# A seven-product first matmul for the third row group of a convolution and MLP kernel

## The chip, the cores and the metric

The kernel runs on one core of one Trainium2 chip. The metric is the device time of one execution in microseconds (us), as the median of the runs. In the profile the engines are called PE (TensorE, matmul), PEld (TensorE's weight load), DVE (VectorE), ACT (ScalarE), POOL or Pool (GpSimd) and SP (SyncE).

## The reference

The input x has shape (8, 4224, 192) in float32. First, a causal convolution with 7 taps runs along the sequence; the taps are a softmax over the kernel axis, one set for each of 8 heads of 24 channels. Its output is then normalised and sent through a two-layer MLP with a residual:

```python
w = exp(weight - max(weight)); w = w / (sum(w) + 1e-9)        # (8 heads, 7 taps)
y[b, s, h, :] = sum over k of w[h, k] * x_pad[b, s + k, h, :]  # 6 zero rows ahead of the sequence
xn  = (y - mean(y)) / sqrt(var(y) + 1e-6) * g_ln               # over the 192 channels
out = y + max(xn @ w_ch1, 0) @ w_ch2                           # 192 -> 768 -> 192
```

## The kernel before

**Rows and groups.** A partition holds 32 consecutive rows of a sequence (the rows that are left over, 8 on every partition, form one group over all sequences). The work goes through groups of up to 16 rows a partition. Group 0 has 6 rows, group 1 the 8 left-over rows, group 2 (the third group) 10 rows, and each later group 16. All pools that matter here have one or two buffers, so groups overlap only where the order of instructions lets them. The order is written by hand: each engine executes its instructions in the order of the source (`tc.manual_schedule()`), and semaphores keep the data dependencies.

**The convolution.** `load_x(g)` fetches a group with six rows of lead. `first_tap` multiplies by tap 0 on ACT into `y`, `second_tap` multiplies by tap 1 on ACT into `tb`, and `add_second_tap` adds `tb` onto `y` with accumulating DMAs issued by Pool. `conv` does the remaining taps on DVE (L417), one instruction for each tap and head: a multiply-add of 24 channels by the rows of the group, 384 elements a partition for 16 rows. `transpose` (L428) turns `y` in blocks of 32 into `yt`, `moments` (L448) takes the statistics on DVE, and `root` computes the inverse deviations on Pool with 22 small operations. The deviation is applied after the second matmul, since it commutes with the ReLU; the mean is taken out of `w1` beforehand.

**Two matmuls in float32.** "Up" multiplies by `w1` (192 x 768) and "down" by `w2` (768 x 192). Up contracts over 32 channels a row group of PE, four row groups side by side, each with a PSUM bank of its own (`rows_of_tiles`, L533). PSUM has 8 banks; `take_set` hands out banks 0-3 or 4-7 in turn and `take_bank` single ones, both from one counter.

Groups 0 and 1 do both matmuls plainly (`up`, and `down` with L772 and the evictions L783/L786). Groups 3 and later use Winograd's form of Strassen's scheme in both: the operands are cut into quarters, sums of quarters are formed, and seven products replace eight. `up_mixed` does this for up: `sums_of_y` forms the sums of quarters of `yt` (s1, s2 on DVE, s3 and s4 on Pool, where s4 overwrites the quarter a21), `w1sums` holds the sums of quarters of `w1`, and the parts c11, c12, c21, c22 of the hidden layer are evicted from PSUM by ACT (L642) and completed by accumulating DMAs (`add_by_dma`, L609), by a DVE addition that reads PSUM (L648) and by ReLUs on ACT (L655). `down_fast` does it for down (L835): the half sums on DVE (L802), evictions on ACT (L841), and a list `work` of ACT instructions that are put behind the matmul chunks; `behind` says how many go behind each chunk of each product. `finish_fast` adds and transposes the result back (L897, L899).

Group 2 before the change does up plainly, in six chunks of 128 hidden units with an eviction each (L523), and down with `down_fast`. Around it, before the change, the source orders (stage g is the turn of the main loop):

- Stage 0, behind the statistics: Pool forms `w1sums[1]` and `w1sums[0]` (L582).
- Stage 1: `conv(2, 2)` on DVE, the transposition of group 2, `first_tap(3)`, the DMAs of group 3's second taps (6 heads), the four `w2sums` on Pool, `load_x(4)` and `store_y(2)` by Pool, then `down(1)`; then the statistics of group 2, its `root` on Pool, and `conv(3)` for heads 6 and 7.
- Stage 2: `up(2)`, with the scaling of group 0's outputs, the accumulating output DMAs of groups 0 and 1 (`add_to_out`) and the first taps of group 4 put between its chunks (`between`); then `conv(3)` for heads 0 to 5, `lower_sum(2)` between two parts of it, `w1sums[2]` on Pool, and `down_fast(2)`. In there DVE transposes group 3 and subtracts two quarters of `w1` in place (L870).

`let_in` writes one element of a tile on DVE; whatever writes that tile next on Pool waits for it, so Pool starts there no earlier than DVE has come to that place.

`room` is one large tile that holds the hidden layer (`ht`) of all groups in turn, and at its end the second taps of group 3 (`tb[3]`).

Of the kernel before, what the change touches and what calls it, by code (L numbers as in the profile page):

```python
# [16 lines left out]
def kernel(  # L17
# [69 lines left out]
    FC = NF // 2  # L87

# [295 lines left out]
    def second_tap(g, heads=(0, H)):  # L384
# [7 lines left out]
        elif g == 3:  # L392
            tb[g] = room[:, (NF * NQ * C - D) * J :].rearrange("p (j d) -> p j d", d=D)
        else:
            tb[g] = bpool.tile([P, J, D], F32, tag="tb", name=f"tb{g}")
# [97 lines left out]
    def hidden_tile(g):  # L493
        n = groups[g][2]

        if fast[g]:
            ht[g] = room.rearrange(
# [41 lines left out]
    def between(g, f):  # L539

        if g == 1 and f > 2:
            second_tap(3, heads=[(0, 2), (2, 5), (5, 6)][f - 3])
        elif g == 2:
            if f == 0:
                scale(0, 0, groups[0][2])
                add_to_out(0, 0, groups[0][2])
                nc.gpsimd.memset(xg[4][0:1, 0:PAD, :], 0.0)
            elif f == 2:
                add_to_out(1, 0, groups[1][2])
            elif f > 2:  # L550
                first_tap(4, heads=[(0, 3), (3, 6), (6, 7)][f - 3])
# [34 lines left out]
    def quarters_of_y(g):  # L586
        if width(g) == C:
            cuts = [(slice(HJ * h, HJ * h + HJ), slice(0, C)) for h in range(2)]
# [4 lines left out]
    def sums_of_y(g, engine):  # L593

        room = upool.tile([P, 3 * HJ * CH * C], F32, tag="ys", name=f"ysums{g}")
        room = room.rearrange("p (v j c t) -> p v j c t", v=3, c=CH, t=width(g))
# [11 lines left out]
    def add_by_dma(dst, src):  # L608
        nc.gpsimd.dma_start(out=dst, in_=src, accum_op=ALU.add)  # L609

# [195 lines left out]
    def lower_sum(g, fs=range(FC)):  # L806

        a = of_products(g)
        if g in MIXED:
# [8 lines left out]
    def down_fast(g, work):  # L818
# [9 lines left out]
        banks = [take_bank() for c in range(CH) for i in range(2)]  # L828
# [22 lines left out]
        if g == 2:  # L851
            work += [lambda h=h: first_tap(4, heads=(h, h + 1)) for h in range(7, H)]
# [6 lines left out]
        behind = (1, 1, 1, 1) if g == 2 else (3, 2, 2, 3)  # L859
# [6 lines left out]
        if g + 1 < NG:  # L866
            transpose(g + 1)
            if g == 2:
                b11, b12 = quarters_of_w1()[0:2]
                nc.vector.tensor_tensor(b12, b12, b11, op=ALU.subtract)  # L870
# [3 lines left out]
        for c in range(CH):  # L874
# [3 lines left out]
            )  # L878
        product(0, a[:, 1, 1], w2sums[:, 1], parts[0], False, 2)
# [111 lines left out]
    for g in range(NG):  # L991
# [3 lines left out]
        if mixed:  # L995
            work = up_mixed(g, ahead(g), pending)
            pending = iter(())
        else:
            up(g)
            work = []  # L1000
        if g == 0:
# [17 lines left out]
            sums_of_quarters(w1sums[:, 0], w11, w1sums[:, 1])  # L1019
            next(root(0, True))  # L1020
        elif g == 1:
            conv(2, 2)
            transpose(2)
            first_tap(3)
            add_second_tap(3, 6)
# [65 lines left out]
```

## Time and profile before

| what | value |
|---|---|
| median of 3 runs | 958.18 us (957.67 to 958.47) |
| the profiled execution's own time | 959.62 us |
| its span in the profile | 957.5 us |
| PE busy | 950.6 us (99%) |
| DVE busy | 890.7 us (93%) |
| ACT busy | 696.6 us (73%) |
| Pool busy | 338.4 us (35%) |
| granted PE clock | 1.0 throughout |
| first matmul of group 2 | 81.64 to 101.23 us |
| second matmul of group 2 | 101.23 to 118.67 us |

The profiled execution took 959.62 us, of which the profile's span covers 957.5; the other 2.1 lie around it. All positions in the span are in us from its start. A row of the timeline gives start, duration, engine, source line, operation, output and inputs, shape and how often; what stands in brackets is how long the engine was idle before it and who ended that. The duration of a group runs from the first start to the last end, and neighbouring instructions overlap a little, so a step's price is taken from start to start. A float32 matmul appears as two records, so a round of four row groups is 8 records.

### The profile page before, as it was taken

To read this page: it belongs to the slowest core of one execution; us is meant where nothing else is said; L and a number is where in the kernel's file an instruction comes from. 1 tells how busy PE (TensorE), PEld (TensorE's weight loads), DVE (VectorE), ACT (ScalarE), POOL (GpSimd) and SP (SyncE) were. 2 spreads that over 40 slices of the span, in tenths; PEclk is the share of its full clock that TensorE was granted. 3 is DMA by queue.
4 is the path that set the end of the run, shared out by engine and by line. 5 is a ranking of instruction groups with operands and counts; after the bars stand their busy time and mean duration, and the time that the engine had idled before them with its cause. 6 is when DMAs were issued, how large, how long until landed. Compare 5 with 4: busy or idle time off the path is not lost.

```text
span 957.5 us, 37878 instructions
## 1 busy us (share of the span) xinstructions
PE 950.6 (99%) x16858; PEld 743.1 (78%) x16858; DVE 890.7 (93%) x1489; ACT 696.6 (73%) x1165; POOL 338.4 (35%) x472
## 2 busy tenths in 40 slices
PE   9999999999999999999999999999999999999998
PEld 8998896876869697787968778695867769586787
DVE  7999999999999998999999999999999999999757
ACT  6853678596877959687795968779695877967462
POOL 1058422623145141533227141452316232261310
PEclk9999999999999999999999999999999999999999
DMA  8359589689697988979697896969889696778251
GB/s 204 101 160 212 98 230 280 121 187 229 135 263 138 249 156 181 224 132 277 127 249 151 196 220 127 278 131 252 155 197 205 124 276 132 175 136 138 42 96 68
DMA packets 39544, 168.82 MB, mean 176 GB/s; under 512 B 4437, under 2 KB 8150, under 8 KB 33367
## 3 DMA queue, kind: packets, MB, share of 16 engines
q0 software_dynamic: 32576, 106.25, 59.8%
q1 hardware_dynamic: 6800, 60.16, 17.3%
q8 instruction: 132, 2.16, 0.9%
q14 instruction: 30, 0.25, 0.1%
q10 hardware_dynamic: 6, 0.00, 0.0%
HBM read 38.93 MB, written 50.33 MB: 93 GB/s over the span
## 4 chain that ended last, share of the span: by engine, by line
PE 97%; POOL 1%; DMA 1%; ACT 0%; issue 0%; DVE 0%; ACTq 0%; POOLq 0%
PE ps L533 47%; PE ps L835 44%; PE ps L772 4%; PE ps L367 1%; DMA room<-room 1%; PE ps L326 1%; ACT room L642 0%; POOL room L609 0%; POOL d L460 0%; PE ps L354 0%; POOL r L483 0%; POOL d L479 0%; DVE yt L428 0%; POOL d L478 0%; PE ps L335 0%
## 5 line engine op out<-in xcount | busy, mean ns | idle before, releaser
L417 DVE SCALAR_TENSOR_TENSOR y<-xg,taps,y 128x384 f32<-128x384 f32 (+3 forms) x720 | 364.8, 583 | 1.9 <-DMA y<-room 1.3
L835 PE MATMUL ps<-room,w2sums 128*32 128x256 f32 (+2 forms) x4608 | 247.4, 371 | 0.0
L533 PE MATMUL ps<-yt,w 32*128 32x256 f32 (+2 forms) x4104 | 234.8, 378 | 0.3 <-DVE yt L428 0.3
L642 ACT COPY room<-ps 128x1024 f32<-128x1024 f32 (+1 forms) x135 | 175.0, 1296 | 78.6 <-PE ps L533 77.8
L533 PEld LDWEIGHTS ps<-yt,w 32*128 32x128 f32 x4104 | 204.1, 185 | 25.8 <-issue 8.7
L835 PEld LDWEIGHTS ps<-room,w2sums 128*32 128x32 f32 x4608 | 153.5, 110 | 87.8 <-ACT room L655 5.3
L835 PE MATMUL ps<-room,w 128*32 128x256 f32 (+2 forms) x3456 | 189.8, 371 | 0.1
L802 DVE TENSOR_TENSOR room<-room 128x1024 f32<-128x1024 f32 (+2 forms) x147 | 161.2, 1172 | 22.7 <-PE ps L835 16.1
L835 PEld LDWEIGHTS ps<-room,w 128*32 128x32 f32 x3456 | 113.9, 110 | 67.9 <-DVE room L648 5.0
L533 PE MATMUL ps<-ysums,w1sums 32*128 32x256 f32 x2160 | 125.3, 379 | 0.2 <-issue 0.2
L533 PEld LDWEIGHTS ps<-ysums,w1sums 32*128 32x128 f32 x2160 | 109.1, 185 | 11.2 <-ACT room L642 3.6
L925 POOL DMA_DIRECT2D out_dram<-ot x69 | 58.9, 940 | 159.3 <-ACT ot L914 102.6
L409 POOL DMA_DIRECT2D y<-tb x59 | 52.4, 1384 | 155.0 <-ACT room L841 110.2
L841 ACT COPY cs<-ps 128x256 f32<-128x256 f32 (+2 forms) x192 | 70.2, 367 | 45.6 <-PE ps L835 45.5
L655 ACT ACTIVATE room<-room 128x1024 f32<-128x1024 f32 (+1 forms) x89 | 92.5, 1072 | 0.8 <-DMA room<-parts_cs 0.8
L914 ACT ACTIVATE ot<-ot,r 128x192 f32<-128x192 f32 x224 | 90.9, 464 | 0.0
L380 ACT ACTIVATE y<-xg,taps 128x384 f32<-128x384 f32 (+3 forms) x141 | 73.1, 608 | 0.2 <-DMA xg<-in_x_dram 0.2
L448 DVE BATCH_NORM_STATS2 st<-y 128x6 f32<-128x192 f32 x264 | 70.1, 344 | 0.0
L841 ACT COPY room<-ps 128x256 f32<-128x256 f32 (+2 forms) x96 | 35.5, 369 | 46.5 <-PE ps L835 43.8
L398 ACT ACTIVATE tb<-xg,taps 128x384 f32<-128x384 f32 (+1 forms) x120 | 66.0, 627 | 0.0
L533 PE MATMUL ps<-yt,w1sums 32*128 32x256 f32 x1080 | 65.3, 380 | 0.4 <-ACT room L642 0.4
L533 PE MATMUL ps<-ysums,w 32*128 32x256 f32 x1080 | 64.6, 376 | 0.0
(113 smaller groups left out, 918.0 us busy)
## 6 DMA issues: line engine op xcount, KB each, us to landing
xg<-in_x_dram SPq DMA_DIRECT2D x14, 2112.0 KB, 16.6
room<-room POOLq DMA_DIRECT2D x45, 512.0 KB, 5.1
out_dram<-ot POOLq DMA_DIRECT2D x59, 384.0 KB, 9.6
y<-tb POOLq DMA_DIRECT2D x58, 384.0 KB, 8.5
out_dram<-y SPq DMA_DIRECT2D x13, 1536.0 KB, 9.5
room<-parts_cs POOLq DMA_DIRECT2D x28, 512.0 KB, 6.8
room<-parts_tb POOLq DMA_DIRECT2D x14, 1024.0 KB, 7.6
xg<-in_x_dram POOLq DMA_DIRECT2D x1, 2112.0 KB, 13.6
```

The source lines that it names most:

```text
L380: nc.scalar.mul(y[g][:, 0:n, cs], xg[g][:, 0:n, cs], taps[:, h, 0:1])
L398: nc.scalar.mul(tb[g][:, 0:n, cs], xg[g][:, 1 : 1 + n, cs], taps[:, h, 1:2])
L417: nc.vector.scalar_tensor_tensor(out=y[g][:, 0:n, cs], in0=t[:, k : k + n, cs], scalar=taps[:, h, k : k + 1], in1=y[g][:, 0:n, cs], op0=AL ...
L448: nc.vector.bn_stats(out=sums[g][:, j, :], in_=y[g][:, j, :])
L533: nc.tensor.matmul(banks[:, q, i * w : i * w + w], right[rows, c, P * i : P * i + P], left[rows, :, c, :], start=(first and c == 0 and i = ...
L642: nc.scalar.activation(dst, src, AF.Relu) if relu else nc.scalar.copy(dst, src)
L655: nc.scalar.activation(c, c, AF.Relu)
L802: nc.vector.tensor_tensor(a[:, *dst, f], a[:, *left, f], a[:, *right, f], op=op)
L835: nc.tensor.matmul(dst[C * q : C * q + C, 0:w], right[:, f, C * c : C * c + C], left[:, f, q], start=(first and f == PAIR), stop=(f == PAI ...
L841: nc.scalar.copy(to[:, c], dst[:, 0:w].rearrange("p (j t) -> p j t", t=t))
L914: nc.scalar.mul(ots[g][:, j, :], ots[g][:, j, :], rstd[g][:, j : j + 1])
L925: nc.gpsimd.dma_start(out=rows[:, d0:d1], in_=src[:, d0:d1], accum_op=ALU.add)
```

## The change

The change gives group 2 a first matmul of seven products (`up_whole`) and orders the work around it anew:

- `up_whole(2)` replaces `up(2)`. Each half of the rows has 5 rows, so a product is 160 columns wide. Its parts are evicted by ACT; c11 and c22 are completed by one accumulating DMA each, c21 by an addition on DVE that reads PSUM. Group 4's memset, `root(2)`, the output DMAs of groups 0 and 1, the first taps of group 4 and parts of `conv(3)` stand between the products.
- The sums of quarters it needs: `w1sums[2]` is formed on DVE in stage 0 instead of on Pool in stage 2; the in-place subtraction of `w1` quarters goes from DVE in `down_fast(2)` to Pool in stage 1; `sums_of_y(2)` is new in stage 1.
- In stage 1, Pool's first three `w2sums` are let in at the transposition, ahead of the second taps' DMAs, and the fourth goes to the end; the DMAs carry 5 heads instead of 6, and the scaling of group 0's outputs comes ahead of `down(1)`.
- Group 3's transposition in `down_fast(2)` is done in two parts, the second behind the half sums; the banks of `down_fast` are assigned in another order; `behind` is (1, 1, 2, 2) for group 2.
- The hidden layer of group 2 lies at another place of `room` (FROM_2), and `tb[3]` is smaller.

```diff
+    FROM_2 = 2 * FC * NQ * J * T - FC * NQ * (J - 6) * C
...
         elif g == 3:
-            tb[g] = room[:, (NF * NQ * C - D) * J :].rearrange("p (j d) -> p j d", d=D)
+            tb[g] = room[:, NF * J * P - n * 5 * GRP :].rearrange("p (j d) -> p j d", d=5 * GRP)
...
         if g == 1 and f > 2:
-            second_tap(3, heads=[(0, 2), (2, 5), (5, 6)][f - 3])
-        elif g == 2:
-            if f == 0:
-                scale(0, 0, groups[0][2])
-                add_to_out(0, 0, groups[0][2])
-                nc.gpsimd.memset(xg[4][0:1, 0:PAD, :], 0.0)
-            elif f == 2:
-                add_to_out(1, 0, groups[1][2])
-            elif f > 2:
-                first_tap(4, heads=[(0, 3), (3, 6), (6, 7)][f - 3])
+            second_tap(3, heads=[(0, 2), (2, 4), (4, 5)][f - 3])
...
+    def up_whole(g):
+        n = groups[g][2] // 2
+        w = n * C
...
+        Y, X = take_set(), take_set()
...
+        def close(c, banks, pool, tag):
+            part = pool.tile([P, J * D], F32, tag=tag, name=f"parts_{tag}{g}")
+            part = part[:, 0 : FC * NQ * w]
+            nc.scalar.copy(part.rearrange("p (f q w) -> p f q w", f=FC, q=NQ), seen(banks))
+            add_by_dma(c.rearrange("p f q w -> p (f q w)"), part)
+
+        def relu(c, f):
+            nc.scalar.activation(c[:, f], c[:, f], AF.Relu)
+
+        rows_of_tiles(X, a11, b11, True, False, True)
+        nc.scalar.copy(c11, seen(X))
+        rows_of_tiles(Y, a12, b21, True, True, True)
+        close(c11, Y, cpool, "cs")
+        nc.gpsimd.memset(xg[4][0:1, 0:PAD, :], 0.0)
+        rows_of_tiles(X, s2, t[0], False, False, True)
+        nc.scalar.copy(c21, seen(X))
+        rows_of_tiles(Y, s3, t[1], True, False, True)
+        nc.scalar.copy(c22, seen(Y))
+        first_tap(4, heads=(0, 1))
+        rows_of_tiles(X, s1, b12, False, False, True)
+        close(c22, X, bpool, "tb")
+        next(root(2, True))
+        for k in range(2):
+            add_to_out(k, 0, groups[k][2])
+        first_tap(4, heads=(1, 2))
+        rows_of_tiles(Y, a22, t[2], False, True, True)
+        conv(3, 2, 5, heads=(0, 5))
+        conv(3, 5, 6, heads=(0, 3))
+        nc.vector.tensor_tensor(c21, c21, seen(Y), op=ALU.add)
+        rows_of_tiles(X, s4, b22, False, True, True)
+        for f in (PAIR, *range(PAIR)):
+            relu(c11, f)
+        nc.scalar.activation(c12, seen(X), AF.Relu)
+        lower_sum(g, (PAIR, *range(PAIR)))
+        conv(3, 5, 6, heads=(3, 5))
+        conv(3, 6, K, heads=(0, 5))
+        work = [lambda h=h: first_tap(4, heads=(h, h + 1)) for h in range(2, 5)]
+        work += [lambda f=f: relu(c22, f) for f in (PAIR, *range(PAIR))]
+        return work + [lambda h=h: first_tap(4, heads=(h, h + 1)) for h in range(5, H)]
...
-        banks = [take_bank() for c in range(CH) for i in range(2)]
+        banks = [take_bank() for i in range(2 * CH)]
+        banks = [banks[c + CH * i] for c in range(CH) for i in range(2)]
...
-        behind = (1, 1, 1, 1) if g == 2 else (3, 2, 2, 3)
+        behind = (1, 1, 2, 2) if g == 2 else (3, 2, 2, 3)
...
-        if g + 1 < NG:
+        if g == 2:
+            transpose(g + 1, 0, CH)
+        elif g + 1 < NG:
             transpose(g + 1)
-            if g == 2:
-                b11, b12 = quarters_of_w1()[0:2]
-                nc.vector.tensor_tensor(b12, b12, b11, op=ALU.subtract)
...
+        if g == 2:
+            transpose(g + 1, CH, NC)
         product(0, a[:, 1, 1], w2sums[:, 1], parts[0], False, 2)
...
             sums_of_quarters(w1sums[:, 0], w11, w1sums[:, 1])
+            nc.vector.tensor_tensor(w1sums[:, 2], w21, w1sums[:, 0], op=ALU.subtract)
             next(root(0, True))
         elif g == 1:
             conv(2, 2)
+            let_in(w2sums[:, 2])
             transpose(2)
             first_tap(3)
-            add_second_tap(3, 6)
+            scale(0, 0, groups[0][2])
             sums_of_quarters(w2sums[:, 2], b12, b22)
             sums_of_quarters(w2sums[:, 0], b12, b11)
             sums_of_quarters(w2sums[:, 1], b22, w2sums[:, 0])
-            sums_of_quarters(w2sums[:, 3], b21, w2sums[:, 1])
+            add_second_tap(3, 5)
             load_x(4, nc.gpsimd, pad=False)
             store_y(2, nc.gpsimd)
-        elif g == 2:
-            conv(3, 2, 5, heads=(0, 6))
-            lower_sum(2)
-            conv(3, 5, K, heads=(0, 6))
-            let_in(w1sums[:, 2])
-            sums_of_quarters(w1sums[:, 2], w21, w1sums[:, 0])
+            sums_of_y(2, nc.gpsimd)
+            moments(2)
+            sums_of_quarters(w12, w12, w11)
+            sums_of_quarters(w2sums[:, 3], b21, w2sums[:, 1])
         if g < 2:
             down(g)
             if g == 1:
-                moments(2)
-                next(root(2, True))
-                conv(3, heads=(6, H))
+                conv(3, heads=(5, H))
             continue
```

More of the change, by code (lines that the diff above doesn't have):

```diff
@@ L496, in hidden_tile @@
         if fast[g]:
-            ht[g] = room.rearrange(
+            start = 0 if g in MIXED else FROM_2
+            ht[g] = room[:, start : start + NF * NQ * n * C].rearrange(
                 "p (h e f q j t) -> p h e f q j t", h=2, e=2, f=FC, q=NQ, t=width(g)
@@ L587, in quarters_of_y @@
         if width(g) == C:
-            cuts = [(slice(HJ * h, HJ * h + HJ), slice(0, C)) for h in range(2)]
+            n = groups[g][2] // 2
+            cuts = [(slice(n * h, n * h + n), slice(0, C)) for h in range(2)]
         else:
@@ L595, in sums_of_y @@
         room = upool.tile([P, 3 * HJ * CH * C], F32, tag="ys", name=f"ysums{g}")
+        room = room[:, 0 : 3 * groups[g][2] // 2 * CH * C]
         room = room.rearrange("p (v j c t) -> p v j c t", v=3, c=CH, t=width(g))
@@ L609, in add_by_dma, with seen @@
         nc.gpsimd.dma_start(out=dst, in_=src, accum_op=ALU.add)
+    def up_whole(g):
+        n = groups[g][2] // 2
+        w = n * C
+        assert FC * w <= 512
+        hidden_tile(g)
+        a = of_products(g)
+        (c11, c12), (c21, c22) = [
+            [a[:, h, e].rearrange("p f q j t -> p f q (j t)") for e in range(2)] for h in range(2)
+        ]
+        a11, a12, a21, a22 = quarters_of_y(g)
+        s1, s2, s3, s4 = ysums[g]
+        b11, b12, b21, b22 = quarters_of_w1()
+        t = [w1sums[:, k] for k in range(3)]
+        Y, X = take_set(), take_set()
+        def seen(banks):
+            return banks[:, :, 0 : FC * w].rearrange("p q (f w) -> p f q w", w=w)
+        def close(c, banks, pool, tag):
[35 more added lines that the diff above has]
+        return work + [lambda h=h: first_tap(4, heads=(h, h + 1)) for h in range(5, H)]
@@ L808, in lower_sum @@
         a = of_products(g)
-        if g in MIXED:
+        if g > 1:
             for f in fs:
@@ L851, in down_fast @@
         if g == 2:
-            work += [lambda h=h: first_tap(4, heads=(h, h + 1)) for h in range(7, H)]
             work += [lambda h=h: second_tap(4, heads=(h, h + 1)) for h in range(H)]
@@ L997 @@
             pending = iter(())
+        elif g == 2:
+            work = up_whole(g)
         else:
```

## The prediction, made before the changed kernel was run

> **What bounds the kernel now.** I read the page's busy shares first, then the chain that ended last, then the stage table (busy time by windows), then the timeline of the two stages that the change rewrites. The chain is TensorE (PE) almost from end to end:
>
> ```profile
> PE 950.6 (99%) x16858; PEld 743.1 (78%) x16858; DVE 890.7 (93%) x1489; ACT 696.6 (73%) x1165; POOL 338.4 (35%) x472
> ```
>
> ```profile
> 30.33 7.86 PE ps L533 x192
> ...
> 50.09 15.75 PE ps L533 x288
> 65.84 15.80 PE ps L772 x96
> 81.64 19.59 PE ps L533 x288
> 101.23 17.44 PE ps L835 x504
> ...
> 229.88 27.96 PE ps L533 x504
> ```
>
> Start, duration, records: 81.64 is the third group's first matmul (the stage rewritten), 101.23 its second. PE stands still nowhere there, so PE work taken away is time gained only if every other engine hands over earlier by as much. VectorE (DVE) is the one to doubt. The stage table (window, its length, then PE, PEld, DVE, ACT, POOL busy) shows it nearly full in just this stage:
>
> ```profile
> 65.80:81.60 15.80, 15.80 (x104) 15.57 (x100) 15.70 (x30) 7.70 (x17) 10.50 (x13) 1.00 0.65 65
> 81.60:101.20 19.60, 19.60 (x293) 14.67 (x295) 18.27 (x34) 11.94 (x19) 13.90 (x26) 1.00 0.97 242
> ```
>
> The timeline shows how DVE meets GpSimd (Pool) there, and the two places where an eviction or DVE stands right ahead of PE:
>
> ```profile
> 72.67 3.16 POOL L582 TENSOR_TENSOR w2sums<-w 128x288 f32<-128x288 f32 x2
> 73.59 4.80 DVE L417 SCALAR_TENSOR_TENSOR y<-xg,taps,y 128x384 f32<-128x384 f32 x4
> 75.91 2.07 POOL L582 TENSOR_TENSOR w2sums<-w,w2sums 128x288 f32<-128x288 f32 x2
> ...
> 81.67 0.73 ACT L786 ACTIVATE ot<-ps,r 128x192 f32<-128x192 f32 x2 [3.17 <-PE ps L772]
> ...
> 93.49 2.29 DVE L802 TENSOR_TENSOR room<-room 128x640 f32<-128x640 f32 x3
> ...
> 144.59 2.29 DVE L648 TENSOR_TENSOR room<-room,ps 128x2048 f32<-128x2048 f32 x1 [1.22 <-PE ps L533]
> ...
> 125.78 9.57 DVE L417 SCALAR_TENSOR_TENSOR y<-xg,taps,y 128x384 f32<-128x384 f32 x18
> ```
>
> One convolution step alone is 9.57/18 = 0.53 us (start to start). The four beside the Pool subtractions took 4.80 instead of 2.13: DVE lost 2.67 us.
>
> **1. The products.** Before: 6 chunks x 6 x 4 row groups; four row groups run at once, so 36 rounds of 320 columns (288 records, 8 a round): 19.59/36 = 0.544 us. After: 7 products x 3 x 3 = 63 rounds of 160. Rounds measured here: 0.328 at 192 columns (7.86/24), 0.438 at 256 (15.75/36), 0.544 at 320, a straight line through nearly zero (0.0017 a column), which gives 0.273 at 160. The second matmul of this very group has 63 rounds of 160 in 17.44, 0.277 with its product boundaries; I take that: 17.45. **Gain 2.14.** The Trainium skill (TensorEngine Tiling (Array Packing), Performance Considerations, Instruction Overhead) speaks against it: about 60 cycles of overhead for each matmul. With 27 more rounds of two matmul instructions at 2.4 GHz that would take back some 1.35 us (an estimate from that page) and leave about 1.1 of an ideal 2.5; the rows, on a line through nearly zero, do not show it.
>
> **2. First bank.** The new stage calls take_set twice and writes its first product to the second set, X. Counting the calls (the set counter stands at 4 after down(1)), X is banks 0-3, which down(1) has just filled; before, the first chunk took 4-7. Bank 3 is freed by the two L786 evictions, 81.67 to 82.40, and the fourth row group of the first round waits for it. **Loss 0.8** (0.76 plus a handover). The scaling of the first outputs now stands ahead of those evictions on ScalarE (ACT): 6 x 0.36 = 2.2 us at 71, while ACT idles 3.17 before each pair, so nothing.
>
> So PE ends the seven products at 81.64 + 0.8 + 17.45 = 99.9.
>
> **3. DVE up to the closing of c21.** Second matmul's first product now goes to banks 4-6, which the DVE addition into c21 reads; PE cannot start it before that ends. Step by step:
> - w1sums[2] moves from Pool to DVE, ahead of conv(2,2), which starts at 53.12. It needs Pool's w1sums[0], which ends at 51.12 + 2.63 = 53.75; start 53.85, then 1.3 (L870, same shape, 1.32). Everything after is **2.0 later**.
> - The transposition ends at 71.0 + 2.0 + 0.1 (the gating memset) = 73.1. The sums s1, s2 (480 elements) are 0.65 each (L897, 128x480, 0.65), waiting some 0.2 for Pool: 74.65. Ten statistics of 0.26 (2.66): 77.25.
> - conv(3): heads 5-7, 18 steps; heads 0-4 of three taps, 15; 3 more. 36 x 0.53 = 19.05, to 96.3 if Pool is silent (30 steps before; the 1.33 that DVE waited for the second taps at 83.95 is gone, since it comes there later).
> - Pool is not silent. From 71.1 it has three subtractions of 288 (0.75 each, beside the transposition, which shares nothing: 3.38 us with Pool's L582 beside it at 102, 3.38 without at 154), two second-tap DMAs (1.96 for both at 70.8), load_x(4) and store_y(2) (0.6 each), and only at 76.5 s3, a21 (480 each), w12 (1152) and w2sums[3] (288). All but 0.7 us of s3 falls beside conv(3): about 2100 elements. Price: DVE lost 2.67 while Pool did 4 x 288 = 1152, 2.3 ns an element, which is Pool's own pace (2.63/1152). **4.8 us.** Bounds: the last two of the four cost 0.53 each (1.85 ns: 3.6 us for w12, w2sums[3] and a21); three of the four charged with all of it, 3.1 ns: 6.2; and nothing, if Pool fell into the gaps, as root's 32-element operations do. I take the middle: it is the nearest shape.
> - DVE reaches c21 at 101.1; product 6 is done at 97.5. 128x1920 from PSUM by L648: 2.29 x 1920/2048 = 2.15, to 103.25.
>
> So PE starts the second matmul at 103.3, not 99.9: **loss 3.4.**
>
> **4. Inside the second matmul.** lower_sum (2.29 for the three, L802) ends at 105.6, ahead of its product at 105.8: nothing. ACT: c22's three ReLUs are now put behind the chunks of the second product, the last behind the last chunk. Copy of the last chunk (0.17 start to start) and a 640-element ReLU (L655 is 1.07 for 1024, some 0.7 here) end 0.95 after the product does; the third product wants it in its third round, 0.55 in: **loss 0.45**. c22's transfer (copy ends 96.8, 7.6 us to land as L609 from parts_tb) is there at 104.5, ReLU asked for at 106.3: hidden by 1.8. Seven remaining conv steps and half a transposition (1.7) bring DVE to 111, about when half_sum may start (before, it waited 1.72 there): nothing. The w12 subtraction (1.32) is gone from DVE.
>
> **5. Handed on.** The other half of the transposition, 1.7, now lies behind half_sum, ahead of s1/s2, statistics and the next group's conv, with PE-bound half sums ahead of it: DVE reaches L648 at 144.59 later by 1.7 relative to PE, where it had 1.22 idle. PE waits for that addition (it restarts at 146.98, when L648 ends): **loss 0.4**. From there PE and DVE are in step again and later groups idle as before (0.86 at 200).
>
> **6. Queues.** Pool: c11's addition at 89.4, the memset, c22's at 97, then root(2) (22 operations, 9 us before, up to 11.6 between DVE steps) to 108, ten output DMAs (7.8) to 115, second taps of group 4 (3.6) to 119, s3 of group 3 at 122: none waits for another in a way that reaches PE; output DMAs land (9.6) by 125, ahead of the next output tile's first write at about 126.7. load_x(4) goes out 2.5 us earlier: gain for nobody, first_tap(4) asks later. ACT inside the seven products: 1.76 for each eviction (1.01 at 1024, 1.87 at 2048) plus at most 0.55 for a tap, under the 2.5 of a product: nothing.
>
> **Sum:** -2.14 + 0.8 + 3.4 + 0.45 + 0.4 = +2.9 us. On the profiled execution's own time, 959.62 (span 957.5), that is 962.5; that execution stood 1.44 above the median 958.18, so the median becomes **961.1**.
>
> **Rivals.**
> - *Pool costs DVE nothing* (rows for it: 128x32 operations cost no step anything; the transposition). Then c21 is added from 97.5 to 99.65, the stall of 3.4 is about 0.1, the wait for ReLUs 0.6 since ACT has c12 just before: -2.14 + 0.8 + 0.1 + 0.6 + 0.4 = -0.2: 958. Against: the four steps in 4.80.
> - *The other side, faster:* PE's work decides and DVE does not. It needs DVE at c21's closing by 97.5, thus no Pool conflict and the 2.0 at 53 not paid, and ACT's set X free at 81.6. All held, -2.1: 956.0. One mechanism, DVE's slack; it decides where DVE comes to c21 before product 6 ends. The table's 18.27 of 19.60 busy, with 2.15 + 1.3 + 1.3 added, is against it.
> - *c22's addition lands late.* Behind load_x(4) and the rest of the queue it may need the 13.6 of xg's load instead of 7.6; the ReLU then stands in ACT's queue ahead of the evictions, with the fifth x's taps behind it: PE waits some 2 to 4 more: 963 to 965.
>
> **How the numbers follow.** My case, with Pool's price between 3.6 and 6.2, reaches +1.7 to +4.3 and has 0.67; no conflict 0.2; faster 0.05; late landing 0.08. About 0.2% (1.9 us) is what a measurement of this kernel tells from no change: faster below 956.3, slower above 960.1. Faster: 0.05 and a little of the no-conflict case, 0.06. Slower: late landing and nearly all of my case but its low end, 0.65. Same: the rest, 0.29. Range: down to the no-conflict case, 957.6, up to 963.0.
>
> **What would show it.** In the profile after: PE's up stage as 504 records of about 18.3 us from 81.64, its first round broken until 82.4; conv steps of 1 us and longer beside Pool's L582 and the sums from 77 to 85; the c21 addition starting with no idle time before it, at about 101; PE's first L835 released by it near 103.3; a short wait for a ReLU near 109; the next group's L648 without its 1.22 idle. Wrong if the c21 addition waits for PE, or PE goes from L533 to L835 with no gap: then DVE has slack that I did not find. Wrong the other way if ACT's ReLU of c22 waits on a DMA.

## The result, and the profile after

The changed kernel takes 974.72 us (median; 972.15 to 976.55) against 957.93 (957.67 to 958.47) for the kernel before in the same comparison: a ratio of 1.0173 [1.0148, 1.0198], so 16.8 us slower. The prediction was 961.1 us, with 957.6 to 963.0 as its range. The direction was right, the size far off.

The profiled execution is the fastest of the changed kernel, 972.15 us with a span of 970.0. The span grew by 12.5 us against that of the profile before. The first line of the page looks harmless: PE still seems busy nearly all the time.

```profile
PE 954.3 (98%) x17074; PEld 745.8 (77%) x17074; DVE 896.9 (92%) x1495; ACT 703.2 (72%) x1170; POOL 344.9 (36%) x476
```

PE's busy time rose by 3.7 us (950.6 before), though the seven products should have taken 2.1 off; its idle time rose by 8.8. Both have to be explained. The stage table shows where PE idled in group 2 (window, its length, PE, PEld, DVE, ACT and POOL busy, granted clock, DMA share, GB/s; the two matmuls of group 2):

```profile
79.80:101.90 22.10, 18.49 (x507) 17.55 (x507) 21.45 (x35) 12.44 (x12) 6.70 (x13) 1.00 0.78 210
101.90:122.80 20.90, 18.19 (x510) 16.01 (x506) 18.35 (x26) 14.78 (x35) 17.35 (x26) 1.00 0.76 127
```

PE is idle 3.6 us in the first stage and 2.7 in the second; before it stood still in neither. The chain that ended last, further on, shows a loss that is in no idle time (start, duration, records):

```profile
153.55 27.40 PE ps L891 x504
180.96 28.49 PE ps L535 x504
209.44 27.82 PE ps L891 x504
237.26 28.45 PE ps L535 x504
```

L535 is the first matmul, L533 before. The fifth group's lasted 27.96 before and lasts about 28.5 now, and so does that of every later group, none of which the prediction thought touched. From PE's starts, stage by stage:

| stage | before | predicted | after |
|---|---|---|---|
| first matmul, group 2 | 19.59 | 21.65 | 22.05 |
| second matmul, group 2 | 17.44 | 17.9 | 20.90 |
| first matmul, group 3 | 28.38 | 28.8 | 30.76 |
| from there to PE's last stage's end | | +0 | +5.9 |

That is 2.46 + 3.46 + 2.38 + 5.9 = 14.2. The stage of group 2 also began 1.7 earlier in this profile (79.84 against 81.57), which leaves the 12.5 of the span. This is not shown to be a gain of the change: in the profiles of the experiments below, most of them with other code in this place, it began between 79.6 and 81.2, so in the profile before it began later than in any of them.

The timeline of the changed kernel carries the reasons (start, duration, engine, line, operation, output and inputs, shape, count; in brackets the idle time before it and who ended it). The rows come from several windows of it:

```profile
74.88 24.20 DVE L418 SCALAR_TENSOR_TENSOR y<-xg,taps,y 128x384 f32<-128x384 f32 x36
...
80.74 5.02 PE L535 MATMUL ps<-yt,w 32*128 32x160 f32 x137 [0.35 <-ACT ot L841]
...
89.75 2.73 PE L535 MATMUL ps<-ysums,w1sums 32*128 32x160 f32 x72 [1.42 <-issue]
...
96.23 0.82 PE L535 MATMUL ps<-ysums,w 32*128 32x160 f32 x16 [1.85 <-issue]
...
99.63 2.15 DVE L654 TENSOR_TENSOR room<-room,ps 128x1920 f32<-128x1920 f32 x1 [0.55 <-PE ps L535]
...
101.89 2.65 PE L891 MATMUL ps<-room,w 128*32 128x160 f32 x72
...
107.69 0.74 ACT L633 ACTIVATE room<-room 128x640 f32<-128x640 f32 x1 [1.64 <-DMA room<-parts_tb]
...
108.52 0.48 PE L891 MATMUL ps<-room,w2sums 128*32 128x160 f32 x8 [1.54 <-ACT room L633]
...
118.20 3.69 POOL L410 DMA_DIRECT2D y<-tb  x4
...
123.24 2.46 PEld L535 LDWEIGHTS ps<-yt,w 32*128 32x128 f32 x44 [0.15 <-ACT cs L897]
...
133.67 14.90 DVE L418 SCALAR_TENSOR_TENSOR y<-xg,taps,y 128x384 f32<-128x384 f32 x28 [2.51 <-DMA y<-tb]
...
153.55 1.72 PE L891 MATMUL ps<-room,w 128*32 128x256 f32 x28 [2.36 <-DVE room L703]
```

Five things are to be seen. (a) At 89.75 and 96.23 PE stands still for 1.42 and 1.85 us, and what ended that is "issue": the profile shows nothing that it waited for. (b) The c21 addition (L654) waits for PE, the reverse of the prediction, although DVE's 36 convolution steps did take 24.20. (c) At 107.69 the ReLU of c22 waits for c22's accumulating DMA, and PE for the ReLU. (d) Pool issues group 4's second taps only at 118.20, behind `root(2)` and ten output DMAs; the last of them lands at 133.55, `conv(4)` waits for them until 133.67, DVE then comes late to L703, and PE waits 2.36. (e) At 123.24 the first round of group 3's first matmul is broken: two row groups start, and the weight loads of the third wait for an eviction of ACT (L897).

### The profile page after: what moved, and what is told of

The parts are those of the page before. It is cut to its first block, busy times and chain, and to the rows that moved or that the text cites. A ratio compares the mean times of both kernels' runs of the same rounds, so it can differ in the third digit from the quotient of the medians.

```text
span 970.0 us, 38331 instructions
## 1 busy us (share of the span) xinstructions
PE 954.3 (98%) x17074; PEld 745.8 (77%) x17074; DVE 896.9 (92%) x1495; ACT 703.2 (72%) x1170; POOL 344.9 (36%) x476
## 4 chain that ended last, share of the span: by engine, by line
PE 84%; DVE 0%; issue 0%
PE ps L891 42%; PE ps L535 41%; PE ps L827 1%; DVE room L703 0%; DVE y L418 0%; DVE y L985 0%
## 5 line engine op out<-in xcount | busy, mean ns | idle before, releaser
L535 PE MATMUL ps<-yt,w 32*128 32x256 f32 (+2 forms) x4032 | 231.5, 371 | 1.4 <-DVE yt L429 1.0
L535 PEld LDWEIGHTS ps<-yt,w 32*128 32x128 f32 x4032 | 201.3, 185 | 26.5 <-issue 8.9
L857 DVE TENSOR_TENSOR room<-room 128x1024 f32<-128x1024 f32 (+2 forms) x144 | 158.9, 1176 | 23.2 <-PE ps L891 14.2
L535 PE MATMUL ps<-ysums,w1sums 32*128 32x256 f32 (+1 forms) x2304 | 130.6, 374 | 1.4 <-issue 1.4
L535 PEld LDWEIGHTS ps<-ysums,w1sums 32*128 32x128 f32 x2304 | 114.3, 185 | 12.2 <-issue 4.2
L897 ACT COPY cs<-ps 128x256 f32<-128x256 f32 (+2 forms) x192 | 69.9, 366 | 47.5 <-PE ps L891 47.5
L535 PE MATMUL ps<-ysums,w 32*128 32x256 f32 (+1 forms) x1152 | 67.6, 371 | 1.9 <-issue 1.9
L535 PE MATMUL ps<-yt,w1sums 32*128 32x256 f32 (+1 forms) x1152 | 67.8, 374 | 0.0
L897 ACT COPY room<-ps 128x256 f32<-128x256 f32 (+2 forms) x96 | 35.4, 369 | 43.6 <-PE ps L891 41.5
L703 DVE TENSOR_TENSOR room<-room,ps 128x2048 f32<-128x2048 f32 x17 | 38.9, 2288 | 29.4 <-PE ps L535 27.0
```

The costliest lines, as they stand in the source:

```text
L535: nc.tensor.matmul(banks[:, q, i * w : i * w + w], right[rows, c, P * i : P * i + P], left[rows, :, c, :], start=(first and c == 0 and i = ...
L857: nc.vector.tensor_tensor(a[:, *dst, f], a[:, *left, f], a[:, *right, f], op=op)
L897: nc.scalar.copy(to[:, c], dst[:, 0:w].rearrange("p (j t) -> p j t", t=t))
```

## Experiments

The theories after the result were: **B**, the bank order, written for all groups, costs every later group; **I**, PE runs out of instructions (which come by DMA: the page has a queue `q8 instruction`) in narrow matmuls while the DMA engines are full; **Q**, transfers issued late on Pool's queue (c22, second taps) reach PE; **D**, DVE's late closing of c21, as predicted, only covered by I. The rival to I is that something of the new stage holds PE there.

**The bank order only in group 2.** The changed kernel with one guard:

```diff
         banks = [take_bank() for i in range(2 * CH)]
-        banks = [banks[c + CH * i] for c in range(CH) for i in range(2)]
+        if g == 2:
+            banks = [banks[c + CH * i] for c in range(CH) for i in range(2)]
```

> The changed kernel, with the new assignment of PSUM banks in the second matmul kept for the third group alone; all later groups get the old one back. Theory (banks): in the changed kernel each later first matmul takes 28.49 us instead of 27.96, because the last bank that the second matmul evicts (bank 6) is now one of the four that the next first matmul begins in, so its third row group waits for the last eviction; 14 first matmuls (groups 4 to 17) x 0.53 = 7.4 us come back: 974.7 - 7.4 = about 967.3 us, and the stages read 27.96 again. Rival (the later stages are slower for another reason, such as the new place of the hidden layer or more instructions): they stay at 28.49 and the time stays at 972 to 976.

Measured: 967.1 us, ratio 1.0095 [1.008, 1.011] (before 957.82). Some 7.5 of the 16.8 us are gone ((1.0173 - 1.0095) x 958). Its chain has the old length again from the fifth group on:

```profile
182.48 27.96 PE ps L535 x504
210.44 27.59 PE ps L892 x504
238.03 27.96 PE ps L535 x504
```

The costliest groups of the page hide this loss in busy time. Of the changed kernel, then of this one (busy, mean ns | idle before):

```profile
L535 PE MATMUL ps<-yt,w 32*128 32x256 f32 (+2 forms) x4032 | 231.5, 371 | 1.4 <-DVE yt L429 1.0
```

```profile
L535 PE MATMUL ps<-yt,w 32*128 32x256 f32 (+2 forms) x4032 | 223.9, 370 | 1.4 <-DVE yt L429 1.0
```

The number of matmuls and their mean are alike, the idle time is the same, and yet 7.6 us of busy time are gone: a round of which one row group starts late counts as busy.

**The kernel before with the new bank order everywhere**, and nothing else:

```diff
-        banks = [take_bank() for c in range(CH) for i in range(2)]
+        banks = [take_bank() for i in range(2 * CH)]
+        banks = [banks[c + CH * i] for c in range(CH) for i in range(2)]
```

> The kernel before, with only the new assignment of PSUM banks in the second matmul, for all groups. Theory (banks): 15 first matmuls (groups 3 to 17) x 0.53 = 7.9 us: 958.0 + 7.9 = about 966 us, each of these stages 28.49 instead of 27.96. Rival (bank order costs nothing by itself): 958.

Measured: 965.61 us, 1.0084 [1.0067, 1.0101], 7.8 us slower. Group 2's two stages keep 19.59 and 17.44, and the long first matmuls appear in its chain:

```profile
80.11 19.59 PE ps L533 x288
99.70 17.44 PE ps L836 x504
117.14 28.44 PE ps L533 x504
145.58 27.43 PE ps L836 x504
173.01 28.49 PE ps L533 x504
```

So B is shown from both sides. How it works is read from the code and the trace: at the end of `down_fast` the six banks are 4, 5, 6, 7, 0, 1. In the old order the last product's three outputs lie in banks 4, 6 and 0, in the new one in 4, 5 and 6. The next first matmul begins with banks 4 to 7, one for each row group. Before, the bank evicted last, 0, is none of them; now it is 6, and the third row group's first matmul waits for its eviction. The start of the fifth group's first matmul shows it, in the changed kernel and then in the one with the guard (the windows end at 182 and 183.2, so the counts are those of the window):

```profile
180.88 0.30 PEld L535 LDWEIGHTS ps<-yt,w 32*128 32x128 f32 x4 [0.41 <-issue]
...
181.02 0.37 ACT L897 COPY cs<-ps 128x256 f32<-128x256 f32 x1 [0.92 <-PE ps L891]
181.45 0.74 PEld L535 LDWEIGHTS ps<-yt,w 32*128 32x128 f32 x15 [0.26 <-ACT cs L897]
```

```profile
182.41 0.96 PEld L535 LDWEIGHTS ps<-yt,w 32*128 32x128 f32 x20 [0.41 <-issue]
```

Two row groups load their weights (4 records), and the third waits for the eviction that ends at 181.39; with the guard nothing interrupts the loads. The first round splits in two, and so does the second (the stage's matmuls start in two steps more, and four of the steps have two records instead of four); the stage costs 0.53 more (28.49 against 27.96). Fourteen such stages make 7.4. The expectation had counted fifteen, with group 3's first matmul; that one took 28.44 here and 28.38 before.

**Narrow matmuls in the kernel before.** Group 2's plain first matmul is done as two halves of 160 columns instead of one of 320; no seven products and no other order:

```diff
+        for c in range(NC):
+            for h in range(2):
+                for q in range(NQ):
...
+                        banks[:, q, h * w : h * w + w], right[rows, c, :],
+                        left[rows, n * h : n * h + n, c, :], start=(c == 0 and h == 0),
...
+            if g == 2:
+                rows_in_halves(banks, yt[g][:, 0:n], w1[:, :, f * P : f * P + P])
```

> The kernel before, with the third group's first matmul cut into matmuls of 160 columns instead of 320: the same columns in twice the instructions (72 rounds of 0.272 instead of 36 of 0.544), nothing else changed. Theory (instructions): the pauses of 1.4 and 1.9 us between the products of the changed kernel, which lie 256 PE records apart, are PE waiting for its own instructions while the DMA engines are 97% busy; here PE asks for instructions at the same pace over the same DMA load, so pauses of 1 us or more appear inside the stage, 256 records apart, and it takes 21 to 23 us instead of 19.6: 959.5 to 961.5. Rival (those pauses were waits for operands from Pool or for evictions): the stage takes 19.6 to 19.8 and the time is 958.

Measured: 962.11 us, 1.0041 [1.0026, 1.0056]; the stage took 23.44 instead of 19.59, both a little above what was expected. The chain shows it in four pieces, with three pauses between them:

```profile
79.77 7.80 PE ps L546 x218
88.65 4.63 PE ps L546 x128
94.58 4.63 PE ps L546 x128
99.40 3.81 PE ps L546 x102
```

The two pieces in the middle have 128 matmul records each. With as many weight loads that is 256 instructions of PE. Counted in PE's instructions (matmul records, weight loads and waits, from the start of the span, to within one), the pauses come at positions 2243, 2499 and 2755; those of the changed kernel come at 2242, 2499 and 3523, multiples of 256 apart, though the two kernels do different work there. So the pauses belong to the position in the instruction stream and not to a wait of the new stage. The page counts the fetched instructions: `q8 instruction` moved 132 packets (2.16 MB) before and 134 (2.20 MB) after, some 16 KB each. 2.16 MB are 64 bytes for each of PE's 33,716 matmul records and weight loads, so 256 of them make one packet. The packets stand so to the pauses (PE's pause from the last matmul's start to the next one's):

| kernel | packet on q8 at | PE's pause | position | packet to restart |
|---|---|---|---|---|
| changed | 87.47 | 88.04 to 89.75 | 2242 | 2.3 |
| changed | 93.87 | 94.08 to 96.23 | 2499 | 2.4 |
| changed | 115.12 | 116.53 to 117.38 | 3523 | 2.3 |
| before, narrow | 85.69 | 87.28 to 88.65 | 2243 | 3.0 |
| before, narrow | 92.13 | 92.99 to 94.58 | 2499 | 2.5 |
| before, narrow | 97.07 | 98.91 to 99.40 | 2755 | 2.3 |
| before | 89.91 | 0.25, ending 96.20, its usual pitch | 2242 | 6.3 |
| bank order only in group 2 | 157.04 | 158.35 to 159.32 | 5059 | 2.3 |
| bank order only in group 2 | 165.31 | 166.05 to 167.60 | 5315 | 2.3 |

PE goes on 2.3 to 3.0 us after such a packet has moved. (The profiles of all eleven kernels have 35 pauses above 0.4 us at such positions, and each of them ends 2.2 to 3.0 us after a packet.) In the kernel before the packet is there 6 us ahead; a stretch of 256 instructions takes 8.6 us at its 320 columns and 4.3 at 160, so there is less time to be late in. That PE waits for a late packet of instructions is the reading that fits all of this, but theory I has to be put more widely: the last two rows are a stage of 256 columns (the second matmul of group 3, with a DMA share of 1.03 and 1.05 from 161 to 169), and the same stage of the kernel before has a share as high and no pause. What holds a packet up is not in the trace; the next runs bear on it.

**Output DMAs of groups 0 and 1 ahead of the products** (with the bank order guarded as above):

```diff
+        for k in range(2):
+            add_to_out(k, 0, groups[k][2])
         rows_of_tiles(X, a11, b11, True, False, True)
...
         next(root(2, True))
-        for k in range(2):
-            add_to_out(k, 0, groups[k][2])
```

> The first experiment (old bank assignment from group 3 on) with the output DMAs of groups 0 and 1 moved from behind c22's closing to ahead of the first product. Theory (Pool's queue): in the changed kernel the second taps of group 4 stand behind root and ten output DMAs on Pool, land 2.5 us after DVE wants them (conv of group 4 idle 2.5 us), and PE then waits 2.7 us for DVE at the end of group 3's first matmul; with the outputs gone from there the second taps go out some 4 us earlier and both waits go: about 967.3 - 2.7 = 964.6. Rival (the landing is late because the DMA engines are full, wherever the outputs stand, or c22's addition now lands later behind the outputs): 967 or more.

Measured: 965.38 us, 1.0082 [1.0067, 1.0097], an interval that overlaps that of 1.0095; it lies between the expected 964.6 and the rival's 967. The first matmul of group 3 took 28.77, 2.0 less than in the changed kernel. That is no gain of this edit: the guarded kernel has 28.70 already. Its last second taps land at 132.50 instead of 133.55, and its PE begins that stage 1.0 later, which hides the wait all but 0.4. Here Pool waits for ACT and issues the second taps even later (119.53 against 118.63 in the guarded kernel), and yet they have landed by 132.68 and `conv(4)`, at 133.42, doesn't wait for them. But the first stage grew to 24.03, from 22.57 in the guarded kernel: c11's accumulating DMA stands behind ten output DMAs, is issued at 96.74 instead of 87.99, and its ReLU waits.

```profile
104.19 1.99 ACT L633 ACTIVATE room<-room 128x640 f32<-128x640 f32 x3 [3.02 <-DMA room<-parts_cs]
```

So moving the output DMAs ahead made c11's DMA late, and the time is no better than with the guard alone.

**The fifth x and the store of y issued early, by SP** (bank order guarded too):

```diff
             conv(2, 2)
+            load_x(4, nc.sync, pad=False)
+            store_y(2, nc.sync)
...
-            load_x(4, nc.gpsimd, pad=False)
-            store_y(2, nc.gpsimd)
```

> The first experiment (967.1 us) with the load of group 4's x and the store of group 2's y issued by SP right behind group 2's last convolution step, some 4.5 us earlier than by Pool behind three subtractions and the second taps. Theory (PE waits for its instructions because their fetch stands behind data transfers): the transfers are out of the way some 4 us sooner and Pool's sums start 1.2 us sooner, so the pauses of 1.9 and 2.4 us 256 records apart shrink by half or more: 964 to 966. Rival (the pauses come from the pace of the narrow matmuls alone, whatever the DMA engines carry): same pauses, 966.5 to 967.5.

Measured: 963.51 us, 1.006 [1.0045, 1.0075] (before 957.61), 3.6 less than the guarded kernel and a little better than expected. The two transfers land by 80.2 instead of 91.8, and both pauses in the stage are gone. Stretches of 4 us of the changed kernel, then of this one (columns as in the stage table):

```profile
84.00:88.00 4.00, 4.00 (x122) 4.00 (x119) 4.00 (x9) 3.06 (x2) 0.01 (x1) 1.00 0.91 270
88.00:92.00 4.00, 2.58 (x71) 2.34 (x69) 4.00 (x8) 1.76 (x1) 1.93 (x2) 1.00 1.00 315
92.00:96.00 4.00, 2.38 (x71) 2.13 (x63) 4.00 (x9) 2.27 (x2) 0.00 (x0) 1.00 0.73 150
```

```profile
84.00:88.00 4.00, 4.00 (x126) 4.00 (x122) 4.00 (x9) 2.84 (x2) 0.23 (x1) 1.00 0.13 18
88.00:92.00 4.00, 4.00 (x126) 4.00 (x124) 4.00 (x9) 3.16 (x2) 1.42 (x2) 1.00 0.78 158
92.00:96.00 4.00, 4.00 (x126) 4.00 (x124) 4.00 (x9) 3.83 (x6) 0.89 (x2) 1.00 0.48 96
```

With the DMA share (last column but one) at 0.13 and 0.78 instead of 0.91 and 1.00, PE does 126 matmuls in every 4 us; the packets moved at 84.4 and 88.6, over 3 us ahead of PE's coming to their instructions. And now D comes to light, at its predicted place:

```profile
98.03 2.15 DVE L654 TENSOR_TENSOR room<-room,ps 128x1920 f32<-128x1920 f32 x1
100.28 1.01 PE L892 MATMUL ps<-room,w 128*32 128x160 f32 x23 [2.12 <-ACT room L658]
...
131.42 14.90 DVE L418 SCALAR_TENSOR_TENSOR y<-xg,taps,y 128x384 f32<-128x384 f32 x28 [3.82 <-DMA y<-tb]
```

L654 starts with no idle time before it and ends at 100.18; PE, done with its products, starts at 100.28. PE's pause is 2.4 from start to start. The profile names ACT's L658 as the releaser; but in the changed kernel PE starts the same product at 101.89 while L658 still runs (102.01 to 103.79), and what ends last here is the addition. The ReLU of c22 doesn't wait in this run (104.11): its transfer is issued at 95.11 and has landed at 101.72, so its lateness in the changed kernel goes with the pauses and the transfers that this run took out of the stage. Further on, in the second matmul, pauses of 0.43 and 0.71 us are left, at positions 3523 and 3779, where the DMA share is 1.02 and 1.03 (112 to 120). The late second taps cost even more than before: `conv(4)` waits 3.82, and PE 2.7 at L703.

**Without c22's accumulating DMA** (bank order guarded):

```diff
-        close(c22, X, bpool, "tb")
+        part = bpool.tile([P, J * D], F32, tag="tb", name=f"parts_tb{g}")
...
+        nc.scalar.copy(part.rearrange("p (f q w) -> p f q w", f=FC, q=NQ), seen(X))
```

> The first experiment (967.1 us) with c22's accumulating DMA left out, so that part of the hidden layer of group 2 is not completed. Theory (c22 lands late): ACT's ReLUs of c22 wait 1.6 us for the landing and PE waits some 2.5 us for them in the second matmul; without the transfer that stage falls from 20.8 to about 18.3 and the time by 2 to 2.5: 964.6 to 965. Rival (those waits only hide DVE, which comes late to the half sums behind): the time falls by less than 1, to above 966.

Measured: 963.2 us, 1.0055 [1.0038, 1.0072]; 3.9 less than the guarded kernel, and less than was expected. The ReLU has lost its wait; here it is in the guarded kernel and in this one:

```profile
108.76 0.74 ACT L633 ACTIVATE room<-room 128x640 f32<-128x640 f32 x1 [1.56 <-DMA room<-parts_tb]
```

```profile
107.81 0.78 ACT L633 ACTIVATE room<-room 128x640 f32<-128x640 f32 x1
```

The second matmul fell from 20.76 to 19.43 in the profiles: 1.3 us is what the late landing costs there, beside 0.9 that is left (two pauses of 0.54 and 0.64, each less the usual pitch) from the place of the ReLUs in ACT's order. The rest of the 3.9 is not in this stage. The profiled execution was the slowest of its kernel, 965.78, so the profile doesn't show what made the others faster; a transfer of 960 KB less on the DMA engines would fit I, but that is only argued.

**All of it mended at once**: the early x by SP, the old bank order everywhere, products begun in the other set, c22 closed in three parts, Pool's sums for the second matmul moved behind c22's closing, its `w1` subtraction moved beside the transposition, and `root(2)` back ahead of the stage:

```diff
-        Y, X = take_set(), take_set()
+        X, Y = take_set(), take_set()
+        turn[0] = 8
...
+        for f in (PAIR, *range(PAIR)):
+            nc.scalar.copy(part[:, f : f + 1], seen(X)[:, f : f + 1])
+            add_by_dma(
...
+        sums_of_quarters(w2sums[:, 0], w2q[1], w2q[0])
+        sums_of_quarters(w2sums[:, 1], w2q[3], w2sums[:, 0])
+        sums_of_quarters(w2sums[:, 3], w2q[2], w2sums[:, 1])
...
-        banks = [take_bank() for i in range(2 * CH)]
-        banks = [banks[c + CH * i] for c in range(CH) for i in range(2)]
+        banks = [take_bank() for c in range(CH) for i in range(2)]
...
+            load_x(4, nc.sync, pad=False)
+            store_y(2, nc.sync)
...
+            next(root(2, True))
```

> The changed kernel with what the runs point to mended at once: old bank pairs for all groups; the first product in banks 4 to 7, which down(1) has not just filled; x of group 4 and y of group 2 issued early by SP; c22 closed in three parts; Pool's subtraction of the w1 quarters beside the transposition, three of the w2 sums behind c22's closing, and group 2's root ahead of the products, so that fewer Pool subtractions lie beside convolution steps. If the theories are right together, the first matmul takes 17.6 to 19 us (before: 19.6), the second 17.5 to 18.5, and the time is 957 to 959.5, at best 1 us under the kernel before. Rival (instruction fetch sets the pace whatever the order): pauses of 3 us in all remain in the first matmul and the time is 960 to 962.

Measured: 959.71 us (956.79 to 961.66), 1.002 [1.0008, 1.0032]: still no faster than before, and just outside the 957 to 959.5 that was expected. What was mended disappears, 14.7 us in all ((1.0173 - 1.002) x 958): the first matmul takes 18.65, that of group 3 27.92, later ones 27.96, and DVE's 36 steps are cheaper with Pool's sums gone:

```profile
77.17 20.48 DVE L418 SCALAR_TENSOR_TENSOR y<-xg,taps,y 128x384 f32<-128x384 f32 x36
...
98.43 1.37 PE L535 MATMUL ps<-yt,w 32*128 32x160 f32 x32 [0.95 <-issue]
```

What was missed is the second matmul, 20.28 where 17.5 to 18.5 was expected. What is left there is I in part. PE pauses 1.25 us in the first matmul, and 1.01 and 1.03 in the second, at positions 2754, 3011 and 3266. The DMA share is 1.04, 1.03 and 1.09 in the three stretches from 96 to 108; the third pause (109.20 to 110.23) lies behind them, and its packet moved at 107.72. Without the first pause the first matmul would be 17.5, as predicted for the products. Together they are 3.3, less 0.4 for the usual pitch 2.9, more than the 2.1 that seven products save.

**Narrow matmuls in the kernel before, with the early x by SP**: the edits of the third and the fifth experiment on the kernel before.

> The kernel before with the third group's first matmul in 160-column matmuls (962.1 us) and, in addition, group 4's x and the store of group 2's y issued by SP right behind group 2's last convolution step. Theory (the fetch of PE's instructions stands behind data transfers): no pauses, or under 1 us in all, in the first matmul, stage 19.6 to 20.5, time 958 to 959.5. Rival (the pace of narrow matmuls alone outruns the fetch): the pauses of 1.4, 1.6 and 0.5 us stay, 961 to 963.

Measured: 961.34 us, 1.0044 [1.0028, 1.0061] (before 957.4): not distinguishable from 1.0041. The stage took 22.94 instead of 23.44, with pauses of 0.60, 1.86 and 0.49 at the same three positions. The transfers moved, the output DMAs of groups 0 and 1 filled the room (share 0.57 from 84 to 88, then 1.01 and 0.98), and only the pause in the emptier stretch shrank. This is nearer to the rival's expectation than to mine: making one transfer early does not mend it while others take its place. It supports that the DMA load matters where it really falls, but doesn't prove it.

**The early x and the outputs ahead together**, the edits of the fourth and the fifth experiment:

> The kernel with early x (963.5 us) with the output DMAs of groups 0 and 1 moved ahead of the first product. Theory (Pool's queue): there the conv of group 4 waits 3.8 us for its second taps, which Pool issues at 114.5 behind root and ten output DMAs, and PE then waits 3.0 us for DVE at the end of group 3's first matmul; with the outputs ahead the second taps go out some 3 us earlier, that wait falls below 1 us, and the time to 960.5 to 961.5, if c11's addition behind the outputs still lands in time (DVE is behind it anyway). Rival (full DMA engines, not the order, make the landing late): 963 or more.

Measured: 962.47 us, 1.0054 [1.0037, 1.0072]: no measurable difference from 1.006, and above the 960.5 to 961.5 that was expected, nearer to the rival's 963. The second taps are in time, and `conv(4)` and the closing of group 3 no longer hold PE:

```profile
130.32 14.86 DVE L418 SCALAR_TENSOR_TENSOR y<-xg,taps,y 128x384 f32<-128x384 f32 x28
...
150.16 2.15 PE L892 MATMUL ps<-room,w 128*32 128x256 f32 x36 [0.34 <-DVE room L703]
```

First matmul of group 3: 28.77 instead of 31.74, so 3.0 us less. It is not that Pool issues them sooner; the fifth experiment's kernel first, then this one:

```profile
114.51 3.62 POOL L410 DMA_DIRECT2D y<-tb  x4
```

```profile
116.43 3.55 POOL L410 DMA_DIRECT2D y<-tb  x4 [9.86 <-ACT room L898]
```

They are issued 1.9 later, since Pool waits for ACT, and yet landed sooner: the last 11.8 us after it was issued (118.12 to 129.93) instead of 14.9 (116.17 to 131.10). The DMA share from 114 to 118 is 0.04 and 0.11 here, and 0.89 and 0.98 there. So theory Q, that their place in Pool's queue makes them late, is not what this shows: the landing goes with the load of the output DMAs just ahead of them, which is the rival of this run's expectation. But the output DMAs are back in the stage, the share from 88 to 96 is 1.03 and 1.04 (0.78 and 0.48 without them), and pauses of 1.58, 0.5, 1.32 and 1.82 us return. One gain pays for the other loss.

## Why the prediction was right or wrong

The prediction failed where it put the later groups at nothing. Its step 5 ends with "From there PE and DVE are in step again and later groups idle as before"; the runs showed 0.53 us in each of fourteen later first matmuls instead, 7.4 to 7.5 us in all, from the bank order. The steps that failed next are "So PE ends the seven products at 99.9" (pauses of up to 3.9 us, at fixed places of the instruction stream), "hidden by 1.8" (the ReLU of c22 waited 1.64) and "none waits for another in a way that reaches PE" (2.4). Step by step:

**The products (step 1): right.** 17.45 was predicted; 17.5 was measured where PE could run (18.65 with a pause of 1.25 against a pitch of 0.14). The Trainium skill (TensorEngine Tiling (Array Packing), Performance Considerations, Instruction Overhead) states some 60 cycles of overhead for each matmul; the estimate from it, 1.35 us more for the narrow matmuls, is not to be seen here.

**The first bank (step 2): right in kind, a little large.** The first round breaks for 0.64 between starts, some 0.5 net, instead of 0.8.

**c21's closing (step 3): the mechanism right, its effect covered.** The 36 steps lost 24.20 - 19.05 = 5.1 us to Pool, with 4.8 predicted; from PE's start of the stage DVE reached c21 after 19.2 us (99.08 - 79.84), with 19.5 predicted. With Pool's sums moved away the same steps took 20.48. The Trainium skill (SBUF — State Buffer, Who interferes with whom) has the rule: a DVE instruction with two SBUF inputs contends with a GpSimd instruction that reads SBUF, and the one that comes second is blocked wholly. The rows agree in kind: the loss of 5.1 is about the 4.8 us that Pool's 2100 elements take at its pace of 2.3 ns. PE's stall of 3.4 appears as 2.4 in the fifth experiment and not at all in the changed kernel, where the 3.9 us of pauses had made PE later than DVE. That the stage's length (21.65 predicted, 22.05 measured) came out nearly right is thus chance: the step "PE ends the seven products at 99.9" failed, and the pauses took the place of the stall. The sign that the prediction had set for itself, "Wrong if the c21 addition waits for PE", did appear, though not from slack of DVE.

**Inside the second matmul (step 4): failed.** The failed step is "hidden by 1.8". The copy into the transfer's source ended at 98.9 instead of 96.8, since PE had paused twice ahead of it, and the landing took 8.4 instead of 7.6; the ReLU, wanted at 106.05, waited 1.64. In the fifth experiment, without those two pauses and with fewer transfers there, it didn't wait. PE's three pauses there (1.84, 0.59 and 0.64 from start to start) are some 2.7 beyond the usual pitch of 0.12, where 0.45 was predicted; without the transfer some 0.9 remain, so the ReLU term alone was half its size too. The rival "c22's addition lands late" had the mechanism, at 0.08, as something that happens instead of my case and not with it. A pause of 0.8 at position 3523 comes on top. "ACT inside the seven products: nothing" held.

**Handed on (step 5) and queues (step 6): failed.** 0.4 was predicted for the next closing, 2.4 was measured. The step that failed is "none waits for another in a way that reaches PE". Its order of Pool's queue was right, and its times too (second taps ending at 119 predicted, 121.9 measured), but it ended there: it asked when the transfers are issued and when output tiles come free, not when `conv(4)` needs the second taps. It needed them at 131.2; they landed by 133.55, and it went on at 133.7. In the last experiment they were issued later than in the fifth and still landed sooner, with the DMA engines nearly empty (a share of 0.04 and 0.11): the load of the output DMAs counted there, not their place in Pool's queue.

**What no step had: 7.5 us from the bank order.** The prediction read the two changed lines in `down_fast` for group 2 alone, although they stand outside any test of `g`; step 2 counted the calls of `take_set` for one stage and didn't go on to ask which bank the last eviction frees when the next stage begins. "Later groups idle as before" is true of idle time and was still wrong by 0.53 a group.

**What no step had either: PE's instructions.** Up to 3.9 us in the first stage (1.71 and 2.14 from start to start). The trace before had hints: pauses of 0.28 and 0.56 at positions 3267 and 3522, a packet apart and with nobody who ended them; their packets had moved 2.4 and 2.3 us ahead of PE's restart.

The sum after minus before in the profiles: -2.1 (products), +0.5 (first bank), +3.9 (pauses; the c21 stall is under them), +2.7 and +0.7 (ReLUs of c22, one more pause), +2.4 (second taps), +7.4 (bank order in fourteen stages) make 15.5; 14.2 stands in the table, the difference lying in later stages, of which several ran long in the profile before (2.3 in all beyond the usual 27.96 and 27.44; after, 0.9 besides the bank order). The median lies another 2.6 above the profiled execution. The changed kernel's executions spread over 4.4 us, those of the kernel before over 0.8; pauses that vary would do that, but which ones was not seen, as one execution of each kernel has a profile.

## What to carry to other kernels

Follow an edit of a shared helper through every caller, and with rotating PSUM banks ask at each stage boundary which bank the last eviction frees and which row group needs it first: the loss shows as longer busy time, not as idle time. Before matmuls are cut into more and narrower ones, look for pauses of PE that "issue" ended, at equal distances in the instruction stream, and at the DMA share around them: with full DMA engines the instructions came late here in some stages. A moved transfer must be followed to the engine that consumes it, and of several "hidden" costs in one stage the largest covers the others, so mending one shows the next.

## What was not expected of the hardware

PE stood still for 0.5 to 2.1 us at places of its stream that lie 256 instructions apart (128 matmul records and as many weight loads, one packet), in a kernel before that had only its matmuls halved as in the changed one, and went on 2.3 to 3.0 us after an instruction packet of 16 KB had moved. Narrow matmuls alone don't do it: with the same pitch, and a DMA share of 0.13 to 0.78 from 84 to 96, no such pause was above 0.3 in the stage. Full DMA engines alone don't either: the kernel before has a share of 1.01 and 1.05 from 156 to 164 and no pause. Whether the packet is slow on a full engine or asked for too late stays open.
